# Whole-unit VectorE steps of 4096 columns in a fused linear-attention and rational-MLP kernel, with the split between engines and the written order changed

## Chip, cores and metric

One core of one Trainium2 chip. The metric is the device time in microseconds of one execution; a kernel is run several times and the median is taken. Five engines work side by side, each through its own queue in order: PE (TensorE, matrix products), DVE (VectorE, elementwise), ACT (ScalarE, activations and copies), POOL (GpSimd) and SP (SyncE, which here only issues DMAs). POOL also issues DMAs, those that add into their target among them.

## What is computed

The reference is two stages. The first is a gated linear recurrence for each of 4 batches and 8 heads, over 768 steps with head size 48:

```python
f = 1.0 / (1.0 + np.exp(-f_logit))
for t in range(S):
    state = f[:, :, t, :, None] * state + np.einsum('bhd,bhe->bhde', k[:, :, t], v[:, :, t])
    y[:, :, t] = np.einsum('bhd,bhde->bhe', q[:, :, t], state)
```

The second takes y as 3072 tokens of 384 numbers through a two-layer network whose activation is a rational function:

```python
h = x @ w_in                                  # 384 -> 2048
P = a[0] + a[1] * h + a[2] * h*h + a[3] * h*h*h
Q = 1.0 + np.abs(b[0]) * np.abs(h) + np.abs(b[1]) * h*h
out = (P / (Q + 1e-06)) @ w_out               # 2048 -> 384
```

## The kernel before

The work is cut into 12 units of 256 tokens: unit n is batch n mod 4, part n // 4 of the sequence, so a unit needs the state that unit n - 4 left. Each unit goes through the recurrence and then through the network. The hidden 2048 columns of the network are 16 blocks (m) of 128, so a unit's hidden layer is a tile of 128 partitions by 16 x 256 = 4096 columns. Steps take a range of blocks: `8 16` is one half (2048 columns), `0 4` a quarter (1024 columns).

There is no scheduler. A string, ORDER, lists some 860 steps by hand, and every engine gets its instructions in the order in which its steps stand in that string. Waits between engines follow from the data. So an engine that reaches a step whose input isn't there stops, and all later steps of that engine with it. The steps, with the engine and the line of the kernel before:

- Recurrence: `ld` loads (f, k, q issued by SP, v by POOL, L200); `ef`, `ls` exponential and logarithm of the gate (ACT, L278, L283); `cs` running sums (PE, L293); `A` their exponentials (ACT, L309); `xa` scaled k (1) and q (0) (DVE, L315); `T`, `Te` transposes and their copy (PE L327, ACT L337, once DVE L339); `sc`, `mk` scores and mask (PE L352, DVE L360); `vm` a rearranged piece of v (POOL, L367); `kv`, `si`, `ae`, `st` the new state (PE, PE, ACT, DVE, L421 to L449); `yb`, `yi` the output y (PE, L374), `ye` its copy to x (ACT, L439).
- Hidden layer: `h` products for four blocks (PE, L458; `ha`, `hb` the same in two parts, L482), `hy` their copy from PSUM to bf16 (ACT, L488).
- Denominator: `sq` h squared (DVE, L492; `sa` on ACT instead, L496), `ab` the absolute value, as a bit mask (DVE, L500). Their sum is formed in one of three ways: `u` by products with the identity in PSUM (PE, L508), `zv` by an add on DVE (L518), or `zd` by a DMA that adds (POOL issues it, L522). Then a logarithm, `ln` from u (ACT, L513) or `lz` from z (ACT, L526), and `ex`, an exponential that gives 1/Q in the tile qi (ACT, L530).
- Numerator: `p1`, `p2` two linear terms (DVE, L534, L539), `pm` p1 times h squared (DVE, L548), the sum of both by `tv` (DVE, L556) or by `ta`, a DMA that adds (POOL, L552), and `gm`, times qi (DVE, L560).
- Output: `o` products (PE, L570), `oe` copy (ACT or DVE, L577), `so` store (SP or ACT, L583).
- `dz k` issues k dummy products (PE, L302) whose result nobody reads.

PSUM is four slots of two banks; `@i` says which slot a step takes, and it waits until what was in the slot has been read. qi and lq (the logarithm) exist once for all units, z and h2 (the squares) twice, hy and the numerator's tile gall three times. `ld 2 f >mk.0.1` begins only behind step mk 0 1.

## Time and profile before

| | us |
|---|---|
| median of 3 runs | 218.3 |
| lowest and highest | 218.06, 219.33 |
| span of the profiled execution, first to last instruction | 216.3 |
| TensorE, VectorE, ScalarE, GpSimd busy | 203.2, 202.7, 200.8, 81.6 |

The profile has one execution; its own time is not listed apart from its span. The median is 2.0 us above the span. Matmuls are pipelined and their ends are modelled, so TensorE's busy time is an upper bound of the time it could not have done without. Instructions of VectorE and ScalarE overlap their neighbours a little: the time from one start to the next is shorter than the duration listed. The chain of waits is the work that ended last, followed back from the last instruction.

### The profile page before, as it was taken

The page shows a single profiled execution, that of the slowest core. Times are in us where ns is not written, and L with a number is a line of the kernel's source. Part 1 is how long each engine was busy: PE and PEld are TensorE (multiplying, and loading weights), DVE is VectorE, ACT ScalarE, POOL GpSimd, SP SyncE. Part 2 cuts the span into 40 slices and gives each one's busy share as a digit, 9 for nine tenths or more (in the row PEclk, how much of TensorE's full clock was granted, in tenths as well). Part 3 has the DMA queues.
Part 4 walks back from the last instruction along what each step waited for, and adds up shares of the span by engine and source line. Part 5 has one row for each costly group of instructions (what it writes and reads, how often), then busy time and mean ns, then how long its engine had stood idle before and what let it go on. Part 6 is the DMA issues. An engine that isn't in the chain of part 4 may idle for free.

```text
span 216.3 us, 7159 instructions
## 1 busy us (share of the span) xinstructions
PE 203.2 (94%) x3166; PEld 140.1 (65%) x3166; DVE 202.7 (94%) x246; ACT 200.8 (93%) x211; POOL 81.6 (38%) x91
## 2 busy tenths in 40 slices
PE   6989989699799999999999999999999999999993
PEld 2457658468377657658758658668668678676551
DVE  3588999999999999999999999999999999999991
ACT  4746899999999999999999999999999999999991
POOL 5250247120157803014954205954232516433300
PEclk9999999999999999999999999999999999999999
DMA  5999999999598999958999997999889793999863
GB/s 132 248 226 194 243 212 226 207 221 250 136 246 143 231 237 271 149 101 195 197 232 216 211 251 179 173 234 222 160 159 228 142 162 70 170 194 188 154 234 145
DMA packets 60910, 42.13 MB, mean 195 GB/s; under 512 B 51152, under 2 KB 54992, under 8 KB 60880
## 3 DMA queue, kind: packets, MB, share of 16 engines
q0 software_dynamic: 21232, 22.81, 66.0%
q1 hardware_dynamic: 39360, 18.68, 33.7%
q8 instruction: 24, 0.39, 0.7%
q10 hardware_dynamic: 288, 0.20, 0.3%
q14 instruction: 6, 0.05, 0.1%
HBM read 25.17 MB, written 4.72 MB: 138 GB/s over the span
## 4 chain that ended last, share of the span: by engine, by line
ACT 42%; DVE 21%; PE 18%; DMA 8%; issue 6%; POOL 3%; POOLq 0%; ACTq 0%; DVEq 0%
ACT qi L530 11%; ACT hy L488 10%; PE op L570 9%; ACT lq L526 8%; DMA fn<-in_f_logit_dram 4%; DMA z<-h 4%; PE warm L302 3%; DVE gall L548 3%; ACT A L309 3%; DVE scm L360 3%; DVE qkp L315 3%; PE hp L458 2%; DVE gall L560 2%; DVE gall L556 2%; ACT qkT L337 2%
## 5 line engine op out<-in xcount | busy, mean ns | idle before, releaser
L570 PE MATMUL op<-w_out_sb,gall 128*128 128x384 bf16 x384 | 70.1, 326 | 0.4 <-ACT hy L488 0.4
L458 PE MATMUL hp<-xT,w_in_sb 128*128 128x256 bf16 x564 | 65.3, 272 | 1.3 <-ACT xT L439 1.1
L458 PEld LDWEIGHTS <-w_in_sb 128*128 128x128 bf16 x564 | 55.0, 98 | 11.0 <-issue 2.8
L570 PEld LDWEIGHTS <-gall 128*128 128x128 bf16 x384 | 35.5, 98 | 23.6 <-DVE gall L560 0.9
L488 ACT CAST hy<-hp 128x1024 bf16<-128x1024 f32 x48 | 47.4, 1073 | 1.7 <-PE hp L482 1.2
L530 ACT ACTIVATE qi<-lq 128x2048 bf16<-128x2048 f32 (+1 forms) x26 | 46.9, 1845 | 0.0
L367 POOL COPY vmp<-vn 128x128 bf16<-128x128 bf16 x24 | 33.7, 1417 | 32.1 <-DMA vn<-in_v_dram 18.9
L526 ACT ACTIVATE lq<-z 128x2048 f32<-128x2048 bf16 (+1 forms) x20 | 36.9, 1846 | 0.6 <-DMA z<-h 0.5
L552 POOL DMA_DIRECT2D gall<-hy x17 | 14.8, 926 | 50.7 <-ACT A L309 11.5
L522 POOL DMA_DIRECT2D z<-h x18 | 17.3, 1065 | 36.3 <-issue 10.5
L560 DVE TENSOR_TENSOR gall<-gall,qi 128x2048 bf16<-128x2048 bf16 (+1 forms) x26 | 29.6, 1143 | 0.3 <-ACT qi L530 0.2
L548 DVE TENSOR_TENSOR gall<-gall,h 128x2048 bf16<-128x2048 bf16 (+1 forms) x26 | 29.4, 1138 | 0.0
L492 DVE TENSOR_TENSOR h<-hy 128x2048 bf16<-128x2048 bf16 (+1 forms) x26 | 27.3, 1059 | 1.5 <-ACT hy L488 1.4
L360 DVE TENSOR_TENSOR scm<-sc,mask 128x1024 bf16<-128x1024 f32 x24 | 28.4, 1211 | 0.0
L309 ACT ACTIVATE A<-cs 128x768 f32<-128x768 f32 (+1 forms) x26 | 19.6, 816 | 0.0
L500 DVE TENSOR_SCALAR z<-hy 128x2048 uint16<-128x2048 uint16 (+1 forms) x28 | 17.1, 618 | 0.1
L534 DVE TENSOR_SCALAR gall<-hy,a_sb 128x4096 bf16<-128x4096 bf16 (+1 forms) x14 | 16.9, 1210 | 0.2 <-ACT hy L488 0.2
L539 DVE TENSOR_SCALAR hy<-hy,a_sb 128x4096 bf16<-128x4096 bf16 (+1 forms) x14 | 16.6, 1184 | 0.0
L200 POOL DMA_DIRECT2D vn<-in_v_dram x12 | 13.2, 1104 | 2.2 <-PE y L374 2.2
L315 DVE TENSOR_TENSOR qkp<-kn,A 128x768 bf16<-128x768 f32 (+1 forms) x13 | 11.5, 887 | 2.0 <-ACT A L309 2.0
L278 ACT ACTIVATE fn<-fn 128x768 f32<-128x768 f32 (+1 forms) x13 | 10.7, 825 | 2.8 <-DMA fn<-in_f_logit_dram 2.7
L337 ACT COPY qkT<-tp 128x1024 f32<-128x1024 f32 (+1 forms) x12 | 12.5, 1041 | 0.7 <-PE tp L327 0.7
(72 smaller groups left out, 262.2 us busy)
## 6 DMA issues: line engine op xcount, KB each, us to landing
gall<-hy POOLq DMA_DIRECT2D x16, 512.0 KB, 6.7
z<-h POOLq DMA_DIRECT2D x15, 512.0 KB, 7.4
fn<-in_f_logit_dram SPq DMA_DIRECT2D x11, 384.0 KB, 7.4
kn<-in_k_dram SPq DMA_DIRECT2D x11, 384.0 KB, 9.8
qn<-in_q_dram SPq DMA_DIRECT2D x11, 384.0 KB, 7.2
out_dram<-osb SPq DMA_DIRECT2D x11, 384.0 KB, 4.1
vn<-in_v_dram POOLq DMA_DIRECT2D x12, 192.0 KB, 8.0
w_in_sb<-in_moe_w_in_dram POOLq DMA_DIRECT2D x4, 384.0 KB, 8.2
```

The source lines that it names most:

```text
L309: nc.scalar.activation(t, src, AF.Exp, scale=1.0 if x else -1.0)
L315: return nc.vector.tensor_mul(s["qk"][:, :, x, hh, 0:D], s["qk"[x]][:, hh].rearrange("p h i d -> p i h d"), A_sb[:, :, x].rearrange("p i ( ...
L360: return nc.vector.tensor_mul(t, s["sc", g].rearrange("s r a i t -> s (r a) (i t)"), mb)
L367: nc.gpsimd.tensor_copy(s["vm"][:, :, :, 32 * x:32 * x + 16], src)
L458: nc.tensor.matmul(t[:, m - m0, :], w_in_sb[:, kk, m * P:(m + 1) * P], s["x"][:, kk].rearrange("p i j t -> p (i j t)"), start=(kk == 0), s ...
L488: nc.scalar.copy(fl(big(s, "hy", "hy", 3), m0, m1), fl(s["hp", m0], 0, m1 - m0))
L492: return nc.vector.tensor_mul(fl(big(s, "h2", "h2", 2), m0, m1), fl(s["hy"], m0, m1), fl(s["hy"], m0, m1))
L526: nc.scalar.activation(fl(lq, m0, m1), fl(s["z"], m0, m1), AF.Ln, scale=regs[2], bias=1.0 + 1e-6)
L530: nc.scalar.activation(fl(qi, m0, m1), fl(lq, m0, m1), AF.Exp, scale=-1.0)
L548: return nc.vector.tensor_mul(fl(s["g"], m0, m1), fl(s["g"], m0, m1), fl(s["h2"], m0, m1))
L560: return nc.vector.tensor_mul(fl(s["g"], m0, m1), fl(s["g"], m0, m1), fl(qi, m0, m1))
L570: nc.tensor.matmul(s["op", j][:, j, 0:DM], s["g"][:, m, P * j:P * j + P], w_out_sb[:, m, :], start=(s["on", j] == 1), stop=(s["on", j] == KF))
```

## The change

All functions keep their work, except that `hy` and `ye` may now run on VectorE, which one step uses (`hy 11 4 8 v`). The rest is the ORDER string, which is written anew from the first to the last step. By kind of step and block range it differs so:

| step | before | after |
|---|---|---|
| `sq`, units 2 to 10 | 16 halves (2048 columns) | 9 whole units (4096) |
| `sa` (squares on ScalarE) | 4 quarters (units 2 and 4) | none |
| `ab`, `pm`, `gm`, units 2 to 10 | 18 halves each | 9 whole units each |
| `u` and `ln` | 11 quarters | 9 (unit 2's two are gone) |
| `lz` | 17 halves, 3 quarters | 18 halves, 3 quarters |
| `zd` (by DMA) | 15 halves, 3 quarters | 14 halves, 3 quarters |
| `zv` (on VectorE) | 2 halves (4, 6) | 4 halves (2, 3, 4, 6) |
| `ta` (by DMA) | 16 halves, 1 quarter | 20 halves, 1 quarter |
| `tv` (on VectorE) | 6 halves, 3 quarters | 2 halves, 3 quarters |
| `hy` on VectorE | none | 1 quarter (unit 11) |
| `dz`, in order | 9 5 4 3 1 2 1 1 | 1 4 2 9 1 5 3 1 |

`ex` stays at halves, `p1` and `p2` stay at whole units. In unit 2, blocks 0 to 8 had their denominator by `u`, and have it by `zd` now; blocks 8 to 16 had it by `zd`, and have it by `zv`.

The code, and of ORDER the first and the last lines:

```diff
 ORDER = """
-ld 0 f 2 4; cz 0; ab_ b a; cu 0; cz 1; ld 0 f 0 2; ld 1 f; ci; cu 1; ld 0 v; ld 0 k 0 2; ld 0 k 2 4; fa
-ld 0 q 2 4; ef 0 2 4; ls 0 2 4; cm; ef 0 0 2; dz 9 @2; cs 0 2 4 @2; fr; cz 3; ls 0 0 2; ld 0 q 0 2; ab_ a s
-ld 1 k; dz 5 @3; cs 0 0 2 @3; ef 1; ld 1 q; ls 1; vm 0 1; A 0 1 0 2; wi 12 16 >ls.1; dz 4 @0; cs 1 @0
-A 0 1 2 4; xa 0 1 0 2; A 0 0 2 4; wi 8 12; cz 2; A 0 0 0 2; xa 0 1 2 4; dz 3 @1; kv 0 @2; wi 4 8
-xa 0 0 0 2; si 0 0; ae 0; dz 1 @1; T 0 0 2 @1; wi 0 4; xa 0 0 2 4; st 0 0; Te 0 0 2 s; T 0 2 4 @3; A 1 1
-ld 1 v; Te 0 2 4; A 1 0; vm 0 0; sc 0 0 @1; si 0 1; mk 0 0; sc 0 1 @3; mk 0 1; ld 2 f >mk.0.1; ld 2 k
+ld 0 f 2 4; cu 1; cz 2; ld 0 f 0 2; cz 3; ld 0 k 2 4; cu 0; cz 0; ld 0 q 0 2; ld 0 k 0 2; ld 0 v; cm; ld 0 q 2 4
+ld 1 f; ci; ld 1 k; ld 1 q; ef 0 2 4; ab_ a s; ls 0 2 4; ab_ b a; ef 0 0 2; cs 0 2 4 @2; ls 0 0 2; A 0 1 2 4
+cs 0 0 2 @1; ld 3 f; dz 1 @3; xa 0 1 2 4; A 0 0 0 2; dz 4 @0; cz 1; A 0 1 0 2; A 0 0 2 4; xa 0 0 0 2; xa 0 1 0 2
+vm 0 0; T 0 0 2 @3; ld 1 v; kv 0 @0; xa 0 0 2 4; Te 0 0 2 s; fa; wi 4 8; T 0 2 4 @1; sc 0 0 @3; wi 0 4; ef 1
+Te 0 2 4; ae 0; ls 1; mk 0 0; sc 0 1 @2; cs 1 @1; wi 12 16 >ls.1; mk 0 1; si 0 0; vm 0 1; A 1 1; yb 0 0 2 @3
+st 0 0; fr; yb 0 2 4; ld 2 f >mk.0.1; A 1 0; vm 1 0; xa 1 1; ld 2 k; yi 0 1; wi 8 12; si 0 1; ld 2 q; xa 1 0
...
-zd 11 12 16; o 10 1 4 8; oe 9 0 2 s; p1 11 8 16; o 10 1 0 4; ex 11 4 8; tv 11 4 8; o 10 1 12 16; so 9 0 2 s
-p2 11 8 16; o 10 0 12 16; lz 11 8 12; gm 11 4 8; so 7 0 2 s; o 10 1 8 12; ex 11 0 4; pm 11 8 12
-o 10 0 8 12; pm 11 12 16; so 8 0 2 s; o 11 0 4 8 @1; ex 11 8 12; gm 11 0 4; o 11 1 4 8 @0; lz 11 12 16
-tv 11 8 12; o 11 1 0 4; gm 11 8 12; o 11 0 0 4; ex 11 12 16; tv 11 12 16; o 11 0 8 12; gm 11 12 16
-oe 10 0 2 s; so 10 0 2 s; o 11 1 8 12; o 11 0 12 16; oe 11 0 1 v; so 11 0 1 s; o 11 1 12 16; oe 11 1 2 s
+o 10 1 4 8 @0; ab 11 0 4; o 10 0 0 4; lz 11 12 16; p2 11 0 8; zd 11 0 4; o 10 1 8 12; pm 11 8 12; lz 11 8 12
+o 10 1 0 4; p2 11 8 16; o 10 0 8 12; ex 11 12 16; tv 11 4 8; ta 11 8 12; o 10 0 4 8; pm 11 12 16; oe 9 0 2 s
+o 10 1 12 16; gm 11 4 8; lz 11 0 4; o 10 0 12 16; so 9 0 2 s; tv 11 12 16; so 8 0 2 s; o 11 1 4 8 @2; ex 11 8 12
+gm 11 12 16; o 11 0 4 8 @1; pm 11 0 4; ex 11 0 4; o 11 0 12 16; gm 11 8 12; o 11 1 12 16; oe 10 0 2 s; tv 11 0 4
+o 11 1 8 12; gm 11 0 4; so 10 0 2 s; o 11 0 8 12; o 11 0 0 4; o 11 1 0 4; oe 11 0 1 v; so 11 0 1 s; oe 11 1 2 s
 so 11 1 2 a
 """
...
-    def hy(n, m0, m1):
+    def hy(n, m0, m1, eng="s"):
         s = unit(n)
-        nc.scalar.copy(fl(big(s, "hy", "hy", 3), m0, m1), fl(s["hp", m0], 0, m1 - m0))
+        (nc.scalar.copy if eng == "s" else nc.vector.tensor_copy)(
+            fl(big(s, "hy", "hy", 3), m0, m1), fl(s["hp", m0], 0, m1 - m0))
```

One unit of the middle, as its steps stand in the string (those on VectorE and ScalarE of unit 5's activation alone):

```diff
-ab 5 8 16; sq 5 8 16; sq 5 0 8; ab 5 0 8; p1 5 0 16; pm 5 8 16; pm 5 0 8; lz 5 8 16; p2 5 0 16
-lz 5 0 8; ex 5 0 8; ex 5 8 16; gm 5 0 8; gm 5 8 16
+ab 5 0 16; sq 5 0 16; p1 5 0 16; p2 5 0 16; pm 5 0 16; lz 5 0 8; lz 5 8 16; ex 5 0 8; ex 5 8 16; gm 5 0 16
```

147 lines of the change are left out of this document (71 added, 76 removed).

## The prediction

> **What bounds the kernel now.** I read the page's busy line first, then its chain, then busy time by stages.
>
> ```profile
> span 216.3 us, 7159 instructions
> PE 203.2 (94%) x3166; PEld 140.1 (65%) x3166; DVE 202.7 (94%) x246; ACT 200.8 (93%) x211; POOL 81.6 (38%) x91
> ACT 42%; DVE 21%; PE 18%; DMA 8%; issue 6%; POOL 3%; POOLq 0%; ACTq 0%; DVEq 0%
> ```
>
> Three engines are busy for 93 to 94% of the span, and the chain passes between them: no single one carries it. The stages tell more (columns: length, then busy time of PE, PEld, DVE, ACT, POOL with instruction counts, clock, DMA share, GB/s):
>
> ```profile
> 0.00:16.00 16.00, 13.33 (x170) 6.45 (x170) 9.31 (x35) 9.04 (x16) 7.75 (x20) 1.00 1.06 202
> 16.00:20.00 4.00, 3.87 (x66) 3.20 (x66) 3.27 (x8) 1.81 (x3) 0.00 (x0) 1.00 1.21 192
> 20.00:44.00 24.00, 21.47 (x357) 14.82 (x354) 23.50 (x30) 23.34 (x28) 9.08 (x13) 1.00 1.35 220
> 44.00:190.00 146.00, 141.94 (x2430) 101.41 (x2430) 145.06 (x147) 144.97 (x146) 59.70 (x52) 1.00 0.98 192
> 190.00:211.00 21.00, 20.83 (x142) 13.53 (x140) 20.74 (x30) 20.96 (x20) 5.09 (x6) 1.00 0.87 190
> 211.00:216.30 5.30, 1.79 (x11) 0.70 (x8) 0.82 (x2) 0.71 (x2) 0.00 (x0) 1.00 0.40 148
> ```
>
> From 20 to 211 us VectorE idles 0.50 + 0.94 + 0.26 = 1.7 us and ScalarE 0.66 + 1.03 + 0.04 = 1.7 us of 191; TensorE idles 2.53 + 4.06 + 0.17 = 6.8 us. So VectorE and ScalarE both run without gaps from the end of the start-up to the tail. The time is the start-up, plus the work of the fuller of these two, plus a tail of some 5 us. What an edit saves counts only if it shortens both, and what shortens one alone stops counting when the other is left as the bound. The median of the runs, 218.3, is 2.0 us above this span; I add 2.0 to every span below.
>
> **VectorE's work.** Prices are start to start, from pieces of the chain where instructions follow each other (start, time, what):
>
> ```profile
> 28.69 0.60 DVE h L492
> 29.29 0.34 DVE z L500
> 32.13 0.72 DVE hy L539
> 38.57 2.26 DVE h L492 x2
> 40.83 0.60 DVE z L500
> 52.85 1.13 DVE gall L556
> 56.78 2.26 DVE scm L360 x2
> ```
>
> A two-input step takes 0.60 us for 1024 columns and 2.26 / 2 = 1.13 for 2048: 0.53 per 1024 and 0.07 once. For 4096 that gives 4 x 0.53 + 0.07 = 2.19, against 2.26 for two halves. The one-input AND (L500) takes 0.34 and 0.60, so 0.26 and 0.08: 1.12 for 4096 against 1.20. No 4096-column form of either is in this trace; both are extended along a line. Then, for units 2 to 10:
> - pm and gm: each 18 halves to 9 wholes, 18 x 1.13 - 9 x 2.19 = 0.63 us less, twice: -1.26.
> - ab: 18 x 0.60 - 9 x 1.12 = 0.72 less.
> - sq: 16 halves (two halves were Squares on ScalarE) to 9 wholes: 19.71 - 18.08 = +1.63.
> - zv: two more halves, +2.26. tv: four halves fewer (units 0, 1, 1, 2, 3 to DMA; 7 back), -4.52.
> - hy of unit 11, blocks 4 to 8, comes to VectorE. Not in the trace; the bf16 copy from PSUM below took 0.69, the fp32 multiply from PSUM (L360) 1.13. I take 1.13, since this source is fp32 too.
>
> ```profile
> L339 DVE COPY qkT<-tp 128x1024 bf16<-128x1024 bf16 x1 | 0.7, 691 | 0.7 <-ACT qkT L337 0.7
> L492 DVE TENSOR_TENSOR h<-hy 128x2048 bf16<-128x2048 bf16 x18 | 21.9, 1225 | 0.6 <-ACT hy L488 0.4
> L492 DVE TENSOR_TENSOR h<-hy 128x1024 bf16<-128x1024 bf16 x8 | 5.4, 685 | 0.9 <-ACT hy L488 0.9
> ```
>
> Sum: -1.26 - 0.72 + 1.63 + 2.26 - 4.52 + 1.13 = -1.5 us. As pairs are merged 34 times, everything hangs on what a merge saves. The last two rows give durations: twice 685 less 1225 is 0.145 us, double the 0.07 by starts, because neighbours overlap by about 0.1. I take the starts. [...]
>
> **ScalarE's and TensorE's work.**
>
> ```profile
> 87.37 0.93 ACT h L496
> 88.30 1.82 ACT hy L488 x2
> L513 ACT ACTIVATE lq<-u 128x1024 f32<-128x1024 f32 x11 | 11.3, 1044 | 0.0
> L526 ACT ACTIVATE lq<-z 128x2048 f32<-128x2048 bf16 x17 | 33.6, 1979 | 0.6 <-DMA z<-h 0.5
> 200.49 0.94 PE u L508 x4
> ```
>
> ScalarE loses four Squares (4 x 0.93) and one copy (0.91): -4.6. Two logarithms of 1044 ns become one of 1979: nothing. TensorE loses the two u of unit 2, eight products of 0.94 / 4: -1.9. The 26 dummy products stay, but before, 25 of them ran ahead of unit 0's first hp product; now five (dz 1, dz 4) do, and 21 stand later, where one did: 20 x 0.218 (1.09 / 5, a row of the next part) = +4.4 in the dense part. So TensorE gains 2.5 us of work there against 6.8 us of idle: covered, as long as that idle lies where the dummies fall. VectorE is left as the bound, and -1.5 counts.
>
> **The start.** Steps are taken from the chain and the timeline:
>
> ```profile
> 1.80 4.04 PE warm L302 x9
> 6.67 1.09 PE warm L302 x5
> 6.88 0.84 ACT L278 ACTIVATE fn<-fn 128x768 f32<-128x768 f32 x1
> 7.76 0.84 ACT L283 ACTIVATE lsp<-fn 128x768 bf16<-128x768 f32 x1
> 8.51 1.61 ACT L309 ACTIVATE A<-cs 128x384 f32<-128x384 f32 x4
> 10.71 0.37 PE sv L421 x32
> 11.07 0.28 PE sv L427 x8
> 11.82 0.62 PE tp L327 x8
> ```
>
> ef 1 and ls 1 no longer stand ahead of the four A of unit 0: those begin near 6.9, not 8.51, and everything behind them could come 1.6 us sooner. Against it: the first nine dummies took 4.04 / 9 = 0.449 us each, the next five 1.09 / 5 = 0.218. TensorE begins at half pace, and the nine that bring it up to pace before the first cs are gone. At half pace the two halves of T cost 2 x 0.62 more, kv between them 0.37 + 0.28, and the first sc some 0.3: 2.2 us. Net +0.6. Bounds: -1.6 if TensorE is up to pace anyway, +2.2 if the earlier A doesn't help because q's and k's loads land no sooner.
>
> ```profile
> PEclk9999999999999999999999999999999999999999
> ```
>
> The row of the granted clock shows full pace throughout, so it doesn't separate these; the durations do. [...]
>
> On the queues: POOL now issues v of unit 1 ahead of w_in; h of unit 0 takes blocks 4 to 8 first, whose w_in is now issued first, so they wait on one 384 KB transfer as before. SP issues f of unit 3 early, ahead of f of unit 2, which still waits for mk.0.1. I put these at nothing: h of unit 0 cannot begin before its own x, which comes about as late as before.
>
> **The tail.**
>
> ```profile
> z<-h POOLq DMA_DIRECT2D x3, 256.0 KB, 4.3
> gall<-hy POOLq DMA_DIRECT2D x16, 512.0 KB, 6.7
> L526 ACT ACTIVATE lq<-z 128x1024 f32<-128x1024 bf16 x3 | 3.3, 1093 | 0.0
> L530 ACT ACTIVATE qi<-lq 128x1024 bf16<-128x1024 f32 x4 | 4.2, 1089 | 0.0
> 91.11 3.60 ACT qi L530 x2
> 201.43 11.38 PE op L570 x68
> ```
>
> Unit 11's quarters come in the order 4, 12, 8, 0, and ab of quarter 0 is late. From its end to the last gm VectorE has nine 1024-column steps and two p2 of 2048: 9 x 0.60 + 2 x 0.72 = 6.8 us. In that time zd must land (4.3) and lq, the exponential of quarter 8 and that of quarter 0 must run (3 x 1.09): 7.6, less some overlap. +0.4, bounds 0 and +0.8. Behind the last gm follow two groups of output products, as before.
>
> Three more accumulating transfers of 512 KB (four ta more, one zd less) take 6.7 us each, issued on POOL, which is busy for 38%; where the order puts other work between issue and use they are hidden, and I see no place but the tail where it doesn't.
>
> **Sum.** 216.3 - 1.5 + 0.6 + 0.4 = 215.8, and with 2.0: **217.8**. New waits in the middle I take at nothing over today's 1.7 us; they can lie 1.7 lower and, by the third rival, some 5 higher.
>
> **Rivals.** About 1%, 2.2 us, is what a measurement here can tell from no change: under 216.1 counts as faster, over 220.5 as slower.
> - Faster: the merges save 0.145 rather than 0.07 (34 x 0.075 = 2.5 less), or the start comes 1.6 early (-2.2 against my +0.6), or most of today's 1.7 us of VectorE waits goes because ScalarE now runs 4.6 ahead. One of these gives about 215.2. For it: the durations. Against it: the starts, and that today's few waits leave little to win. 0.24, all of it under 216.1.
> - TensorE becomes the bound: if its 6.8 us of idle lie where nothing can be put, the time changes by its own work, +2.5, plus 2.2 of half pace: 218.3 + 4.7 = 223.0. It decides from the point where less than half of the idle can be used. Against it: the rows show 2.5 us of idle between 20 and 44, near whose end eleven dummies now fall. 0.11.
> - The whole steps gate ScalarE, slower: gm on 4096 columns needs both halves of qi, and holds both until it ends, so the next unit's first exponential waits for 2.2 us of gm where it waited for 1.13, and gm starts up to 1.8 (3.60 / 2) later. ScalarE's 4.6 us of spare cover 0.5 a unit. If VectorE, which has no spare, waits 0.5 us in each of nine units: +4.5, so 217.8 + 4.5 = 222.3. It decides from 0.3 us a unit. For it: every such step is longer than any VectorE step before. Against it: a twelfth of ScalarE's 200.8 us is 16.7, so beside its two exponentials a unit gives it 13 us of other steps to run meanwhile. 0.17.
>
> **Chances.** My case keeps 0.48: within 1%, its terms' bounds reach from 216.2 to 220.4. Faster 0.24, the two slower cases together 0.28. The range runs from 215.0, below the middle of the fast case, to 221.5, into the slow ones, and leaves out about a fifth.
>
> **What would show it.** In the new profile: 4096-column two-input steps near 2.3 us long and 2.19 apart; VectorE's busy sum near 201.2 and ScalarE's near 196; VectorE idle between 20 and 211 us still under 2.5 us and ScalarE's near 5; unit 0's A before 7.2 us and transposes at 0.15 us each; lq of unit 11's last quarter waiting for z's transfer. Wrong would be: VectorE waiting for qi or for hp or sc in the middle (a rival holds), or TensorE with less than 3 us of idle there.

## The result and the profile after

| us | before | after |
|---|---|---|
| median of 4 runs | 218.44 | 224.53 |
| lowest to highest | 218.06 to 219.33 | 223.79 to 226.99 |
| profiled execution: its time, its span | –, 216.3 | 224.98, 223.3 |

The ratio is 1.0282, 95% interval 1.0208 to 1.0356: slower, by about 6 us. 217.8 was forecast, 215.0 to 221.5. Ratios leave out disturbed runs and the medians here don't, so the two can differ a little in what follows.

The page after (span, busy time, the granted clock in 40 slices, the chain by engine):

```profile
span 223.3 us, 7123 instructions
PE 204.9 (92%) x3158; PEld 143.3 (64%) x3158; DVE 200.6 (90%) x211; ACT 196.9 (88%) x205; POOL 78.9 (35%) x94
PEclk9998899999999999999999997999999999999998
PE 35%; ACT 13%; issue 5%; DMA 4%; DVE 4%; POOL 0%; ACTq 0%; DVEq 0%
```

VectorE does 2.1 us less work than before, ScalarE 3.9 less, and the span is 7.0 longer. So the time is in waits, and it must be asked in which stretch. Busy time by stages, before (columns: length, then PE, PEld, DVE, ACT, POOL with counts, clock, DMA share, GB/s):

```profile
0.00:30.00 30.00, 26.57 (x421) 15.96 (x421) 22.08 (x55) 20.19 (x30) 9.97 (x24) 1.00 1.16 211
30.00:60.00 30.00, 26.60 (x477) 18.74 (x477) 30.00 (x33) 29.89 (x35) 9.30 (x13) 1.00 1.20 208
60.00:120.00 60.00, 58.51 (x903) 42.05 (x898) 59.23 (x60) 59.42 (x61) 27.16 (x21) 1.00 1.01 202
120.00:140.00 20.00, 19.65 (x323) 13.41 (x323) 19.93 (x22) 20.00 (x21) 8.86 (x7) 1.00 1.03 196
140.00:211.00 71.00, 70.11 (x1056) 49.25 (x1055) 70.64 (x79) 70.62 (x67) 26.33 (x28) 1.00 0.91 179
```

and after:

```profile
0.00:30.00 30.00, 21.05 (x387) 14.61 (x388) 18.05 (x49) 15.70 (x25) 9.15 (x23) 0.94 1.12 197
30.00:60.00 30.00, 29.44 (x525) 20.67 (x523) 29.96 (x35) 29.55 (x37) 11.24 (x15) 1.00 1.23 242
60.00:120.00 60.00, 59.83 (x1035) 43.11 (x1034) 60.00 (x52) 59.82 (x64) 27.62 (x24) 1.00 1.09 209
120.00:140.00 20.00, 17.95 (x307) 12.83 (x304) 17.00 (x14) 16.37 (x18) 8.97 (x8) 0.91 0.97 185
140.00:211.00 71.00, 68.70 (x877) 47.83 (x866) 68.99 (x55) 69.64 (x58) 21.11 (x25) 1.00 0.88 172
```

Since VectorE's work and its idle time make up the span, the difference can be booked on it. VectorE's idle time changes by +4.03 (0 to 30), +0.04, -0.77, +2.93 (120 to 140) and +1.65 us (140 to 211). Behind 211 us it idles 216.3 - 211 - 0.82 = 4.48 before and 223.3 - 211 - 6.57 = 5.73 after (work there from the same view): +1.25. Together +9.13, less 2.1 of work: +7.0. Two stretches carry 7 of the 9: the first 30 us, and 120 to 140.

**The two stretches.** TensorE's timeline after (start, time, line, what, how many; in brackets the idle time before it and what ended it):

```profile
18.03 0.33 PE L419 MATMUL sv<-ind,lsp 128*128 128x2 bf16 x7
20.43 0.16 PE L419 MATMUL sv<-ind,lsp 128*128 128x2 bf16 x1 [2.08 <-issue]
...
21.14 1.91 PE L319 MATMUL tp<-ident,qkp 128*128 128x128 bf16 x16
...
23.16 1.91 PE L453 MATMUL hp<-xT,w_in_sb 128*128 128x256 bf16 x12
...
130.04 0.28 PE L366 MATMUL y<-scm,vmp 64*32 64x128 bf16 x5
132.37 0.23 PE L366 MATMUL y<-scm,vmp 64*32 64x128 bf16 x3 [2.05 <-issue]
...
132.75 2.28 PE L453 MATMUL hp<-xT,w_in_sb 128*128 128x256 bf16 x12
```

In the midst of eight equal products of `kv` of unit 1, and again in the midst of eight equal products of `yb 8 0 2`, TensorE does nothing for 2 us, and the profile names no engine, no semaphore and no data transfer that ended the wait ("issue"). These are stall 1 and stall 2 below. Behind each of them products run at half pace: twelve hidden products take 2.28 us at 132.75 and 1.91 at 23.16, where the same twelve took 1.47 before. The clock shows it (two windows of after):

```profile
20.60:24.00 3.40, 3.14 (x22) 2.54 (x22) 1.62 (x4) 1.86 (x4) 0.00 (x0) 0.50 1.20 206
133.30:136.70 3.40, 3.40 (x18) 2.26 (x16) 1.31 (x2) 2.00 (x3) 0.14 (x1) 0.50 1.03 230
```

VectorE stands for the state that these products lead to (its timeline):

```profile
21.38 1.02 DVE L444 TENSOR_TENSOR state<-sv,alast 128x384 bf16<-128x384 f32 x2 [2.86 <-PE sv L424]
135.39 0.56 DVE L444 TENSOR_TENSOR state<-sv,alast 128x384 bf16<-128x384 f32 x1 [3.00 <-PE sv L424]
```

The first stretch holds more than stall 1. Unit 0's first hidden products start at 23.16; before it was this row:

```profile
16.99 1.47 PE L482 MATMUL hp<-xT,w_in_sb 128*128 128x256 bf16 x12
```

6.2 us later, then, though VectorE's first mask step began a little sooner than before (13.53 against 13.69). Until 16 us hardly anything is lost (VectorE has worked 8.96 us by then against 9.31); the loss comes between the scores of unit 0 and its hidden layer, where the new order puts the state and transposes of unit 1. The four loads of w_in by issue (its rows in before, then in after: duration, first and last start) and from issue to landing:

```profile
L206 POOL DMA_DIRECT2D w_in_sb<-in_moe_w_in_dram x4: 757/766/769, 9.7 to 11.9; - x4
DMA to landing us min/median/max: 5.7/8.2/10.6
```

```profile
L198 POOL DMA_DIRECT2D w_in_sb<-in_moe_w_in_dram x4: 741/763/775, 12.2 to 17.7; - x4
DMA to landing us min/median/max: 8.1/9.9/10.9
```

The first w_in piece is asked for 2.5 us later and the last 5.8 later, so of the hidden layer's weights none lands before 12.2 + 8.1 = 20.3. Three things thus stand ahead of unit 0's hidden products: unit 1's state and transposes on TensorE, with stall 1 in their midst; `ae 1` ahead of `ye 0` on ScalarE; and these loads. That is read from the order and the landings; the runs of the second and fourth groups below take it apart in part.

**The whole steps themselves** came out as priced (groups by form, after):

```profile
L556 DVE TENSOR_TENSOR gall<-gall,qi 128x4096 bf16<-128x4096 bf16 x9 | 20.6, 2286 | 0.8 <-ACT qi L526 0.7
L544 DVE TENSOR_TENSOR gall<-gall,h 128x4096 bf16<-128x4096 bf16 x9 | 20.5, 2283 | 0.0
L496 DVE TENSOR_SCALAR z<-hy 128x4096 uint16<-128x4096 uint16 x9 | 11.0, 1219 | 0.6 <-ACT hy L483 0.6
```

2.28 us long; start to start in the timeline it is 2.20 to 2.21. And `gm` waited for qi once, 0.7 us in nine units.

**Why TensorE stops in the midst of equal products.** The DMA view has a queue for instructions:

```profile
q8 instruction: 24, 0.39, 0.7%
```

24 fetches, 0.39 MB, 16 KB each: the instruction stream comes in blocks. By the count they are TensorE's: 3158 products and as many weight loads are 6316 instructions, some 263 to a fetch. Between the two stalls TensorE's records count (a window from one to the other)

```profile
20.30:132.20 111.90, 108.80 (x1917) 77.92 (x1916) 108.86 (x107) 107.67 (x120) 46.60 (x44) 0.98 1.13 214
```

1917 products and 1916 weight loads, 3833; with the 7 semaphore instructions of its queue in between, which count as no engine's work, 3840. In the same window the DMA view's row of fetches counts 15 of them (0.25 MB). So a block is 3840 / 15 = 256 instructions, and both stalls stand at the same place of one. The trace has the fetches' times too: the block of stall 2 is fetched at about 130, when a window of half a microsecond around it (129.7 to 130.2) shows it beside accumulating transfers,

```profile
q0 software_dynamic: 22, 0.09, 95.0%
q8 instruction: 1, 0.02, 11.7%
```

and used 2.41 us after its fetch began (129.96 to 132.37), that of stall 1 2.22 (18.21 to 20.43), and no block of after sooner. From the entry of the block ahead to the fetch's begin, counted in blocks from the stalls, it is 4.1 to 5.3 us in after for the fetches at 18, 25, 32, 61, 97, 130 and 137 us, where loads or accumulating transfers fill the DMA engines (share 1.07 to 1.47 in the microsecond around each), and under 1 us, or the fetch even begins before the block is entered, for those at 86, 101, 111, 143 and 149. Of these five the engines are far from full only at 101 and 149 (0.65 and 0.06, against 1.00 to 1.87 at the others), so full engines didn't delay every fetch. The blocks ahead of stalls 1 and 2 were done 4.6 and 4.8 us after they were entered, sooner than delay and fetch together, 6.65 and 6.87; of the others 20 lasted 5.86 us or more, and one of 3.72 was entered after the next one's fetch had begun, and none has such a gap behind it. Ahead of stall 2 lie `yi 8`, `yb 8 2 4` and `kv 9`, all of short products, so its block ran out first. In before no fetch came less than 2.78 us ahead of its use, and there is no such stall. This is the theory called F below: late blocks cost the time. Its rivals: the whole steps themselves cost it (W: they hold buffers and delay what stands behind them on VectorE), or the start does, by TensorE's half pace without the nine dummies (C: unit 0's first eight transposes took 1.03 us, 0.62 in before) or by its order of loads and steps.

### The profile page after: what moved, and what is told of

It is laid out like the page before. It is cut to its first block, busy times and chain, and to the rows that moved or that the text cites. A ratio compares the mean times of both kernels' runs of the same rounds, so it can differ in the third digit from the quotient of the medians.

```text
span 223.3 us, 7123 instructions
## 1 busy us (share of the span) xinstructions
PE 204.9 (92%) x3158; PEld 143.3 (64%) x3158; DVE 200.6 (90%) x211; ACT 196.9 (88%) x205; POOL 78.9 (35%) x94
## 4 chain that ended last, share of the span: by engine, by line
PE 35%; ACT 13%; issue 5%; DMA 4%; DVE 4%; POOL 0%; ACTq 0%; DVEq 0%
PE op L566 15%; PE hp L453 12%; ACT qi L526 5%; DMA z<-h 4%; ACT lq L522 3%; ACT hy L483 3%; PE y L366 2%; PE tp L319 2%; DVE gall L556 2%; PE cs L285 1%; DVE scm L352 1%; PE sc L344 1%; ACT osb L573 1%; PE warm L294 1%; DVE h L488 1%
## 5 line engine op out<-in xcount | busy, mean ns | idle before, releaser
L453 PE MATMUL hp<-xT,w_in_sb 128*128 128x256 bf16 x564 | 69.8, 277 | 0.6 <-ACT hy L483 0.5
L566 PE MATMUL op<-w_out_sb,gall 128*128 128x384 bf16 x384 | 68.6, 326 | 1.5 <-DVE gall L556 1.3
L522 ACT ACTIVATE lq<-z 128x2048 f32<-128x2048 bf16 (+1 forms) x21 | 38.7, 1851 | 0.5 <-DMA z<-h 0.3
L548 POOL DMA_DIRECT2D gall<-hy x21 | 20.4, 1032 | 46.5 <-PE y L366 14.8
L359 POOL COPY vmp<-vn 128x128 bf16<-128x128 bf16 x24 | 24.8, 1084 | 33.3 <-DMA vn<-in_v_dram 27.2
L556 DVE TENSOR_TENSOR gall<-gall,qi 128x4096 bf16<-128x4096 bf16 (+2 forms) x17 | 28.2, 1658 | 1.2 <-ACT qi L526 0.7
L488 DVE TENSOR_TENSOR h<-hy 128x4096 bf16<-128x4096 bf16 (+2 forms) x19 | 28.4, 1505 | 0.0
L544 DVE TENSOR_TENSOR gall<-gall,h 128x4096 bf16<-128x4096 bf16 (+2 forms) x17 | 28.1, 1655 | 0.1
L444 DVE TENSOR_TENSOR state<-sv,alast 128x384 bf16<-128x384 f32 x20 | 10.9, 549 | 7.1 <-PE sv L424 7.1
L329 ACT COPY qkT<-tp 128x1024 f32<-128x1024 f32 (+1 forms) x12 | 12.2, 1020 | 4.6 <-PE tp L319 4.6
L496 DVE TENSOR_SCALAR z<-hy 128x4096 uint16<-128x4096 uint16 (+2 forms) x19 | 15.7, 824 | 0.6 <-ACT hy L483 0.6
L285 PE MATMUL cs<-lsp,Ui 128*128 128x384 bf16 (+1 forms) x39 | 11.1, 344 | 5.2 <-ACT lsp L275 5.2
```

The lines of the kernel that those rows point to most:

```text
L359: nc.gpsimd.tensor_copy(s["vm"][:, :, :, 32 * x:32 * x + 16], src)
L453: nc.tensor.matmul(t[:, m - m0, :], w_in_sb[:, kk, m * P:(m + 1) * P], s["x"][:, kk].rearrange("p i j t -> p (i j t)"), start=(kk == 0), s ...
L488: return nc.vector.tensor_mul(fl(big(s, "h2", "h2", 2), m0, m1), fl(s["hy"], m0, m1), fl(s["hy"], m0, m1))
L522: nc.scalar.activation(fl(lq, m0, m1), fl(s["z"], m0, m1), AF.Ln, scale=regs[2], bias=1.0 + 1e-6)
L544: return nc.vector.tensor_mul(fl(s["g"], m0, m1), fl(s["g"], m0, m1), fl(s["h2"], m0, m1))
L548: nc.gpsimd.dma_start(out=fl(s["g"], m0, m1), in_=fl(s["hy"], m0, m1), accum_op=ALU.add)
```

## Experiments

Eighteen kernels. Each but a_burst, which ran once, carries its ratio to before with the 95% interval; the expectations, quoted, were written before it ran. To shift where blocks end, a step was added that computes nothing that is read; it issues k products of two columns:

```diff
+    def dt(k, sl):
+        t = slot(sl, [P, 2, 512], F32, "tiny")
+        for i in range(k):
+            nc.tensor.matmul(t[0:UB, 0, 0:UB], ind, ind, start=True, stop=True, skip_group_check=True)
```

Each product is two instructions (a weight load and a product: c_layout's 70 bring both counts from 3158 to 3228), so `dt 24` shifts all later block ends by 48.

### First group: moving the block ends

**a_tiny24, a_tiny72, a_tiny104**: after, with 24, 72 or 104 such products in front.

```diff
-ef 0 0 2; cs 0 2 4 @2
+ef 0 0 2; dt 24 @0; cs 0 2 4 @2
```

> Theory F (fetch): TensorE's instructions come in blocks of 256, and the two stalls of 2 us of the changed kernel are two blocks that came late, because the 256 instructions before them were run in under 6.9 us while data transfers held the fetch back by 4.4 us. Theory C: the cold start (the nine warm-up products gone) costs it. Theory W: the whole-unit steps of 4096 columns cost it. Here 24 tiny products (48 instructions, [2 x 2] results that nobody reads) stand at the front of TensorE's order, where it idles. F: every boundary now falls 48 instructions earlier in the work; by the trace of the changed kernel the quickest blocks then end at 17.8, 52.7, 66.1, 127.5 and 168.7 us, so the stalls stay or move: no row that waited at 18.4 or at 130.3 us waits at the same product, others do, 222 to 228 us. C and W: nothing moves, 224.5 +- 0.7 us, with the two stalls in front of the same two products.

> 72 tiny products (144 instructions) in front instead of 24. F: the boundaries fall 144 instructions earlier, where nearly every block takes over 5.6 us of work; one quick block ends at 43 us (3.2 us). The stalls at 18 and 130 us go, at most one of about 1 us appears near 43 us, and the time is 217 to 219.5 us. C: the tiny products are no warm-up of the pace that nine 512-column products are, 223.5 to 225 us. W: 224.5 +- 0.7 us.

> The changed kernel with 104 tiny products (208 instructions) in front; they end before the first sum needs TensorE. By the measured delays and the times of the blocks this is the worst place for the boundaries: stalls of 0.7 to 2 us near 22, 26, 90 and 113 us and one of 4 us or more near 128 us, in the run of small products of units 8 and 9. F: 225 to 231 us. C and W: 224.5 +- 0.7 us.

| kernel | median us | ratio | span | TensorE's gaps by "issue" over 0.5: end (length) |
|---|---|---|---|---|
| after | 224.53 | 1.0282 [1.0208, 1.0356] | 223.3 | 20.4 (2.08), 132.4 (2.05) |
| a_tiny24 | 222.41 | 1.0226 [1.0182, 1.0270] | 219.2 | 68.6 (1.60) |
| a_tiny72 | 224.76 | 1.0289 [1.0237, 1.0340] | 223.8 | 48.2 (1.75), 138.5 (1.59) |
| a_tiny104 | 224.89 | 1.0298 [1.0245, 1.0352] | 223.8 | 28.3 (1.83), 118.1 (1.10), 135.3 (2.10) |

The old gaps go in every case, and new ones open, at the same place mod 256 again. That settles where the gaps come from. It doesn't settle what they cost: the best of the three still has one of 1.60, and the other two are no faster than after. That 72 would leave at most 1 us of gaps was wrong, and so was the gap of 4 us or more that 104 was to open near 128 us: which block is short of time can't be told from the order alone, since the delay of the fetch varies between none and over 5 us.

**a_dz9**: nine dummy products moved from unit 1's activation to the front.

```diff
-ef 0 0 2; cs 0 2 4 @2
+ef 0 0 2; dz 9 @0; cs 0 2 4 @2
...
-A 4 1; dz 9 @3; ta 0 8 16
+A 4 1; ta 0 8 16
```

> The changed kernel with its nine 512-column dummy products moved from about 48 us to the front of TensorE's order, as the kernel before had them. C: the transposes of unit 0 run at full pace again (half their 1.03 us for 8), most of the loss is regained, 217 to 220 us. F: up to 48 us the boundaries fall 18 instructions earlier, which is still inside kv of unit 1, so stall 1 stays some products earlier, and past 48 us they lie where they were within one instruction, so stall 2 stays in yb of unit 7: 223 to 225 us. W: 224.5 +- 0.7 us.

224.25, ratio 1.0273 [1.0225, 1.0321], span 222.5. Stall 1 is gone (up to where the nine stood, block ends lie 18 instructions elsewhere), which F had not expected; stall 2, behind that place, stays, 2.11 up to 131.7. The first transposes run at full pace again (eight in 0.62), and unit 0's hidden products start at 18.96 rather than 23.16. Yet the time is after's, not the 217 to 220 of C. VectorE gains 2.5 us in the first 30; behind gaps of 1.29 and 0.50 at 48 us, where the nine were taken away, the clock is at half from 50.2 to 53.6.

**b_tiny32**: before, with 32 such products in front (and one constant formed earlier, which they read).

```diff
-ef 0 0 2; dz 9 @2; cs 0 2 4 @2
+ef 0 0 2; dt 32 @0; dz 9 @2; cs 0 2 4 @2
```

> The kernel before with 32 tiny products (64 instructions) in front of its nine dummy products (and the two-column indicator that they multiply set first on VectorE instead of later). F: the boundaries fall 64 instructions earlier, where by its trace the quickest blocks end at 144, 175 and 189 us after 4.3, 4.6 and 3.8 us of work, against 5.9 us at the least as it stands: stalls of 0.5 to 1.5 us appear there and the kernel loses 0.5 to 4 us, 219 to 222 us. C and W: no change, 218.4 +- 0.7 us.

218.30, ratio 0.9996 [0.9975, 1.0017]; its longest gap by "issue" is 0.48, at 17.2, at the same place mod 256. A miss: moving the block ends in the order of before opened none of the stalls that were expected at 144, 175 and 189 us. So with the old order late blocks cost nothing here, at either of two placings; why, whether it has fewer runs of short products beside full DMA engines, wasn't tested.

**c_layout**: after, with 30, 8 and 32 such products at three places, meant to put every block end where its block is long.

```diff
-ef 0 0 2; cs 0 2 4 @2
+ef 0 0 2; dt 30 @0; cs 0 2 4 @2
...
-A 4 1; dz 9 @3
+A 4 1; dt 8 @3; dz 9 @3
...
-p2 1 0 16; T 4 @0
+p2 1 0 16; dt 32 @0; T 4 @0
```

> The changed kernel with tiny products put in at three places of TensorE's order: 30 in front, 8 before the nine dummy products at 48 us, 32 before the transposes of unit 4 at 52 us. The places were worked out from the traces so far: at the same time of the work the fetch of a block started the same time after the block before it was entered, whatever kernel it was (about 4 us late at 16 to 26 us, 2 at 34 to 43, 4 at 59 to 66, 0 at 98, 4.5 at 123 to 134, 0 at 138 to 146), and a block was never used within 2.2 us of the start of its fetch; with these places every block has more work before it than its fetch takes, but for two that miss by under 0.5 us. F: no TensorE gap over 0.8 us without a wait, VectorE idle after 30 us under 4 us in sum, 216.5 to 218.5 us. C and W (cold start or whole steps cost it): 223 to 225 us, since all of those are as they were.

224.60, ratio 1.0235 [1.0184, 1.0286]. A miss too, in the range that C and W gave: gaps of 1.07 up to 54.4, 0.81 up to 97.1 and 1.64 up to 138.1.

### Second group: why the block is late, and what a clean run is worth

**a_noacc**: after, without five accumulating transfers between 119 and 127 us (four sums of the numerator, of units 4 and 5, and one of the denominator, of unit 5, are left out).

```diff
-ta 4 0 8
...
-ta 4 8 16
-zd 5 8 16
...
-ta 5 8 16
...
-ta 5 0 8
```

> The changed kernel without the five accumulating DMAs that are issued between 119 and 127 us (numerators of units 4 and 5, half of unit 5's denominator: these sums are left out, and the output of those units is not the reference's). TensorE's instructions and their blocks stay the same. F with the fetch queued behind data transfers: the fetch that started 4.46 us after its block before was entered at 125.5 us starts under 2 us after it, and the stall of 2.05 us in front of the same product in y of unit 8 is gone or under 0.5 us, with the half-pace products after it: 219.5 to 222.5 us. If the lateness of the fetch does not come from these transfers (a fixed rhythm of the sequencer): the stall stays at 2 us, 223.5 to 225 us.

224.0, ratio 1.0257 [1.0208, 1.0307]. TensorE's timeline where stall 2 was, the only row of the DMA view at the block's fetch (126.8 to 127.3), and VectorE's stages:

```profile
131.01 0.22 PE L366 MATMUL y<-scm,vn 64*32 64x128 bf16 x2
131.16 1.48 PE L453 MATMUL hp<-xT,w_in_sb 128*128 128x256 bf16 x12
```

```profile
q8 instruction: 1, 0.02, 16.6%
```

```profile
0.00:30.00 30.00, 20.85 (x386) 14.21 (x387) 17.72 (x49) 15.46 (x25) 9.91 (x24) 0.77 1.15 202
120.00:140.00 20.00, 19.93 (x335) 14.78 (x333) 20.00 (x17) 19.98 (x22) 2.11 (x3) 1.00 0.39 90
140.00:211.00 71.00, 67.74 (x849) 46.56 (x848) 67.73 (x54) 67.72 (x57) 21.22 (x25) 0.98 0.85 164
```

Same order of TensorE, same block end, nothing else on the DMA engines: the fetch begins 0.86 us after its block is entered instead of 4.46, the stall is gone, the twelve products take 1.48 again, and VectorE idles 0.00 us between 120 and 140 instead of 3.00. So the late block of stall 2 is a fetch that stands behind data. The time hardly falls, though: 1.26 of the 3 us are lost again behind 140 (3.27 idle against 2.01), 0.33 in the first 30, where the two kernels are the same, and the profiled span is 0.9 shorter. What a removed stall is worth at its place isn't what the end gains. The time missed the 219.5 to 222.5 that was expected; stall 1 stands there as in after, 2.20 long.

**a_burst**: after, with one step of long hidden products put between the runs of short ones.

```diff
-yb 8 2 4; xa 10 1; kv 9 @0; ab 6 0 16; yb 8 0 2; h 7 12 16 @3
+yb 8 2 4; xa 10 1; h 7 12 16 @3; ab 6 0 16; yb 8 0 2; kv 9 @0
```

> The changed kernel with one thing moved on TensorE and no product added: the hidden-layer products of unit 7's last quarter (12 long products) go ahead of, and the state products of unit 9 (40 small ones) behind, the second half of unit 8's y products. F: the block that ends in the second stall then holds 24 instructions of long products in place of small ones and takes 5.5 to 5.8 us instead of 4.8 us of work; with the delay of 4.46 us and 2.2 us of fetch the stall shrinks from 2.05 to 0.9 to 1.2 us, and the half pace after it need not come; it stands in front of another product, the one with the same place in its block. If the block were not what is waited for, the gap would stay at its product or go with it.

One run: 222.0, span 220.0. The stall is now in `kv 9`, at the same place of the block:

```profile
130.54 0.24 PE L413 MATMUL sv<-vn,qkp 64*64 64x48 bf16 x5
131.66 0.40 PE L413 MATMUL sv<-vn,qkp 64*64 64x48 bf16 x27 [0.88 <-issue]
```

With 1.48 us of products more in the block it falls from 2.05 to 0.88: the block's length against the fetch's delay, 4.46 us in after, decides, as F has it.

**d_layout**: after, with 11, 16 and 6 short products at places chosen from the fetch times of the traces so far; **d_burst** is d_layout with the long step of a_burst ahead of `kv 9`.

```diff
-ef 0 0 2; cs 0 2 4 @2
+ef 0 0 2; dt 11 @0; cs 0 2 4 @2
...
-pm 5 0 16; T 8 @1
+pm 5 0 16; dt 16 @1; T 8 @1
...
-tv 7 8 16; T 11 @2
+tv 7 8 16; dt 6 @2; T 11 @2
```

> Tiny products at three other places, worked out with the delays of all traces so far and with the times of the work as they are when no stall comes ahead: 11 in front (22 instructions), 16 before the transposes of unit 8 at 119 us, 6 before those of unit 11 at 160 us. F: no block comes over 0.6 us late; no TensorE gap over 0.8 us without a wait; what is left late is the start (first k and q, w_in and f of unit 3: VectorE idle up to 30 us 7 to 9 us in sum); 217.5 to 220.5 us. If whole steps or the new order in the dense part cost time of their own (W), the loss stays: 223 us or more with no stalls to see.

> The run before this, and the hidden-layer products of unit 7's last quarter put in front of the state products of unit 9, into the run of 256 small products that the second stall followed. F: the block there takes 1 us longer, the last lateness (0.5 us near 134 us) goes: the same as the run before it or up to 0.7 us less. W: no difference.

d_layout: 223.05, ratio 1.0267 [1.0220, 1.0314], span 220.3, and no gap by "issue" over 0.42. d_burst: 224.11, 1.0282 [1.0245, 1.0318], no gain, with a gap of 1.72 up to 171.7. d_layout is the cleanest test of F on the whole time: its stages, and a row of TensorE's waits,

```profile
0.00:30.00 30.00, 21.35 (x400) 14.54 (x401) 18.95 (x50) 16.41 (x26) 9.07 (x23) 0.89 1.14 201
120.00:140.00 20.00, 19.54 (x342) 14.37 (x340) 19.67 (x17) 19.33 (x21) 8.90 (x8) 1.00 0.98 185
```

```profile
PE sv L418 <- DMA vn<-in_v_dram: 2.1, 1, 2.1
```

Between 120 and 140 VectorE idles 0.33 instead of 3.00, nearly as in before (0.07). The profiled span is 3.0 us shorter than after's, but it is the fastest of six executions (222.07 to 225.53); of the medians' difference, 1.5, no more can be said than that it points the same way, since the two intervals overlap. F had 217.5 to 220.5, so it missed; W had "223 us or more with no stalls to see", and that is what came. Late blocks aren't the whole loss, then.

The first 30 us are nearly as poor as in after (11.05 idle against 11.95). TensorE, which comes to `kv 1` sooner here, waits 2.1 us for v of unit 1, which lands at 17.78, and the clock is at half from 17.0 to 23.9. In after v had landed at 17.4, before `kv 1` began, so stall 1 didn't hide that load. What stall 1 and half pace cost at this place is seen in the kernels that have neither there. From the start of `kv 1` to the first hidden product it takes 5.5 us in after (17.66 to 23.16), 3.5 in d_layout (17.92 to 21.42), but 2.2 in a_tiny24 (17.25 to 19.45) and in c_layout (17.56 to 19.77). The first 30 us of these two:

```profile
0.00:30.00 30.00, 20.15 (x417) 13.85 (x418) 20.65 (x51) 17.51 (x27) 9.70 (x23) 0.94 1.16 204
0.00:30.00 30.00, 21.35 (x427) 14.38 (x428) 20.88 (x52) 17.88 (x28) 9.54 (x23) 0.94 1.13 200
```

VectorE idles 9.35 and 9.12 us there, and 9.1 to 10.2 in a_tiny72, a_dz9 and c_split, which have no stall 1 either, against 11.95 in after and 7.92 in before. **So late blocks, with the half pace behind them, go with the middle stretch, some 3 us of the 7, and with 1.8 to 2.9 of the 4 us at the start; the other 1.2 to 2.3 of these 4 stay in those kernels too.** That is read from single traces by stages; no kernel with the new order is free of late blocks and half pace from end to end, and none has the time back. The nearest by its profiled span is a_tiny24, 219.2, its fastest execution.

### Third group: the whole steps alone

**c_split**: c_layout, with every whole `sq`, `ab`, `pm` and `gm` of units 2 to 10 cut into its halves, at its place.

```diff
-pm 4 0 16
+pm 4 0 8; pm 4 8 16
```

> The run before this with the four whole-unit steps (square, absolute value, product with the squares, product with the inverse) of units 2 to 10 each split into two adjacent halves: 36 more VectorE instructions, nothing else. The prediction's terms (0.07 to 0.08 us saved by each merge, start to start) give 36 x 0.07 to 0.08 = 2.5 to 2.9 us longer VectorE work, and so 1.5 to 3 us more than the unsplit one where VectorE stays the bound. W (whole steps hold ScalarE and TensorE up): faster than the unsplit one.

226.73, ratio 1.0341 [1.0290, 1.0393]: about 1% more than c_layout beside it, 2.1 us by the medians, as the merges' price had it. Busy, c_layout and then c_split:

```profile
PE 203.8 (91%) x3228; PEld 142.5 (64%) x3228; DVE 202.7 (91%) x211; ACT 197.6 (88%) x205; POOL 74.1 (33%) x94
```

```profile
PE 204.1 (91%) x3228; PEld 142.5 (64%) x3228; DVE 204.2 (91%) x247; ACT 198.2 (88%) x205; POOL 75.9 (34%) x94
```

36 instructions more cost VectorE 1.5 us of busy time. Against two halves at the same place, the whole steps are a gain in the new order; that the longer step itself loses the time is refuted.

**b_pm**: before, with the ten `pm` of units 1 to 10 whole, at the place of the second half. **b_merge**: before, with 25 of the pairs whole (8 `pm`, 7 `sq`, 5 `ab`, 5 `gm`), where the second half stood near.

```diff
-pm 1 8 16; ex 1 0 8; h 2 8 12 @3; xa 3 0; h 2 0 4 @0; pm 1 0 8
+ex 1 0 8; h 2 8 12 @3; xa 3 0; h 2 0 4 @0; pm 1 0 16
```

> The kernel before with only the ten products with the squares of units 1 to 10 made whole-unit steps (10 instructions of 2048 columns fewer), in the place of the second half. By the prediction's term (0.07 to 0.08 us each) 0.7 to 0.8 us less VectorE work: 217.3 to 218.0 us. If a longer step in itself makes the short steps behind it late (the masks that TensorE waits for), the gain is lost or turned: 218.5 to 221 us.

> The kernel before with the whole-unit steps alone: 25 pairs of halves (7 squares, 5 absolute values, 8 products with the squares, 5 products with the inverse) that stand near each other in its order become one step each, nothing else moves, TensorE's order and its blocks stay. By the prediction's terms VectorE saves 25 x 0.07 to 0.08 = 1.8 to 2.0 us: 216.2 to 217.2 us. If whole steps make ScalarE or the DMAs wait (W): 218.5 us or more.

b_pm: 220.24, ratio 1.0099 [1.0072, 1.0127], span 217.5, clock full throughout. b_merge: 224.72, 1.0297 [1.0264, 1.0329], span 221.8, clock full. In b_pm the merge pays what was forecast: start to start the `pm` take 2 x 1.184 + 10 x 2.210 = 24.47 us where 22 x 1.143 = 25.15 stood, 0.068 a merge. And yet it is slower; TensorE now has waits for VectorE that before hasn't (its waits):

```profile
PE sv L415 <- DVE qkp L309: 1.3, 2, 1.1
PE y L368 <- DVE scm L354: 1.2, 1, 1.2
```

The scaling step of the first row stands behind a whole `pm` on VectorE and comes 1.06 us later than behind a half. The mask of the second row is 0.7 us late, but for another reason: between 100.9 and 106.7 us VectorE's steps ran slower, one scaling step above all, which took 1.62 us where it takes 0.95 in before,

```profile
100.91 1.62 DVE L309 TENSOR_TENSOR qkp<-kn,A 128x768 bf16<-128x768 f32 x1
```

and a GpSimd copy beside it, from 100.98 on, stands in before too (from 101.19, beside the same step). Why it was slow is open. By the whole trace VectorE's idle time grows by only 0.5 us, to 14.1, and its busy time by 0.7 instead of falling by that much. In b_merge VectorE itself waits, since a whole `sq` or `ab` needs the last of four copies from PSUM (VectorE's waits, and a stage):

```profile
DVE z L493 <- ACT hy L481: 3.4, 3, 1.6
DVE h L485 <- ACT hy L481: 3.1, 4, 1.6
```

```profile
140.00:211.00 71.00, 66.37 (x1031) 47.07 (x1031) 66.40 (x62) 66.94 (x62) 28.44 (x29) 1.00 0.88 165
```

4.6 us of idle where before had 0.36, 6.4 more over the whole span. So whole steps in the old order cost 2 us (ten of them) to 6 us (25); with 25 it is waits, with ten only in part. That an order written anew is what they want is argued from this, not shown: the change's own is slower too.

### Fourth group: the start

All five go out from d_layout, which has neither stall 1 nor stall 2. **d_warm** puts dummies into TensorE's gaps at the start, so that the clock holds; **d_v1** issues v of unit 1 earlier; **d_warmv1** does both; **e_f3** is d_warmv1 with f of unit 3, its gate and its logarithm later; **e_start** is e_f3 with `si 0 0` ahead of `cs 1` as well.

```diff
-ef 0 0 2; dt 11 @0; cs 0 2 4 @2
+ef 0 0 2; dt 3 @0; cs 0 2 4 @2
...
-mk 0 0; sc 0 1 @2
+mk 0 0; dz 3 @2; sc 0 1 @2
...
-ld 3 k; kv 1 @2
+ld 3 k; dz 5 @2; kv 1 @2
```

```diff
-vm 0 0; T 0 0 2 @3; ld 1 v; kv 0 @0
+ld 1 v; vm 0 0; T 0 0 2 @3; kv 0 @0
```

```diff
-cs 0 0 2 @1; ld 3 f; dz 1 @3
+cs 0 0 2 @1; dz 1 @3
...
-ld 2 q; xa 1 0
+ld 2 q; ld 3 f; xa 1 0
...
-mk 1 0; ef 3; h 0 0 4 @0; mk 1 1; ls 3
+mk 1 0; h 0 0 4 @0; mk 1 1
...
-hy 1 12 16; cs 3 @0
+hy 1 12 16; ef 3; ls 3; cs 3 @0
```

```diff
-sc 0 1 @2; cs 1 @1; wi 12 16 >ls.1; mk 0 1; si 0 0
+sc 0 1 @2; si 0 0; cs 1 @1; wi 12 16 >ls.1; mk 0 1
```

> d_layout with 8 of the 11 tiny products in front replaced by 512-column dummy products where TensorE idles at the start: 3 before the second half of unit 0's scores, 5 before the state products of unit 1, which wait for v; the count of instructions ahead of every later block is the same. Theory H (half pace): the granted clock stays at 1.00 up to 30 us, the transposes of unit 1 take 1.0 us instead of 1.91 and the hidden products 1.3 instead of 2.66: VectorE idle up to 30 us falls from 10.7 to 8 to 9 us, 220.5 to 222 us. Theory V (the load): the state products still begin at 17.5 to 18.5 us; no gain over 0.5 us.

> d_layout with the load of v of unit 1 put ahead of the copy of unit 0's v in GpSimd's order, so that it is issued near 4.5 us instead of 9.6 to 11.3. V: v of unit 1 lands by 13 us, its state products begin near 16 us with no wait for it; the loads of unit 0's k and q land up to 1 us later in exchange; net 1 to 2 us less, 221 to 222 us. H: begins earlier, but still at half pace: less than 1 us.

> Both edits of the two runs before. If the load and the half pace both cost, their gains add up: 2.5 to 4 us less than d_layout, 219 to 220.5 us, with VectorE idle up to 30 us near 7 to 8 us as in the kernel before. If w_in, which lands at 20 us and later, is next behind them, the gain stops at 1 to 2 us and TensorE waits for w_in at 20 us.

> d_warmv1 with the load of f of unit 3 and its two ScalarE steps put later: the load behind q of unit 2, the steps in front of that unit's sums. Loads hold the start: w_in's first pieces land 1 to 2 us earlier, ScalarE no longer waits for f at 24 us, VectorE idle up to 30 us falls from 9.8 to 8 to 9 us: 1 to 2 us less than d_warmv1 (whose runs were 221.3 to 224.7). If something else holds it: no change beyond 0.5 us.

> The run before this, and the first identity product of unit 0's state put ahead of unit 1's sums on TensorE, which wait for f of unit 1: the state of unit 0 (VectorE waits 1.4 us for it at 16 us) comes about 1 us earlier; 0.5 to 1 us less than the run before it if nothing else is late there, no change if the masks or v are.

| kernel | median us | ratio | unit 0's hidden products from | VectorE busy by 60 us |
|---|---|---|---|---|
| before | 218.44 | | 16.99 | 52.1 |
| after | 224.53 | 1.0282 [1.0208, 1.0356] | 23.16 | 48.0 |
| d_layout | 223.05 | 1.0267 [1.0220, 1.0314] | 21.42 | 48.95 |
| d_warm | 224.57 | 1.0291 [1.0239, 1.0343] | 20.28 | 49.4 |
| d_v1 | 226.24 | 1.0219 [1.0147, 1.0291] | 19.98 | 47.5 |
| d_warmv1 | 223.82 | 1.0260 [1.0218, 1.0302] | 21.52 | 49.7 |
| e_f3 | 225.36 | 1.0282 [1.0236, 1.0327] | 21.85 | 46.1 |
| e_start | 225.77 | 1.0349 [1.0304, 1.0395] | 21.98 | 47.05 |

None regains the start. d_warm holds the clock at 1.00 from end to end, and VectorE idles 9.58 us in the first 30 instead of d_layout's 11.05, so half pace costs up to 1.5 us there (v of unit 1 also landed 0.8 sooner); 1.0 of it is lost again by 60 us, where a late block makes a gap of 0.96 up to 55.3, and a gap of 1.57 up to 172.0 follows, since its products move block ends too. The median gains nothing. In a_noacc, above, half pace lies over `kv 1` as well, and VectorE idled only 0.33 more than in after. In d_v1, whose trace is of a long execution (227.87; its four are 221.85 to 228.8), v of unit 1 lands at 13.5 and `kv 1` waits no more, but begins at 17.77 all the same, and then unit 3's gate, which lands at 25.0, holds ScalarE, and VectorE stands behind it (VectorE's waits):

```profile
DVE h L493 <- ACT hy L488: 2.6, 1, 2.6
```

e_f3 takes that load back, and q of unit 1 (2.2 us, up to 19.4) and the running sums (2.6 us between 34 and 37) are late instead. Each edit lifts one wait, and the next load in the queue stands in its place. By 60 us every one of these has done 2.4 to 6 us less of VectorE's work than before. So what late blocks and half pace leave of the start's loss is one of the order, of loads against first uses. One sign of it: in d_warm, as in a_dz9 and c_split, the first hidden products wait for w_in, 0.2 to 0.6 us, which lands between 18.9 and 20.2 there and at 15.4 in before. Which part belongs to `kv 1`, to `ae 1` ahead of `ye 0` and to w_in's later issue stays open. Moving unit 0's `ye` and hidden products ahead of unit 1's state, the edit that the landings suggest, wasn't tried.

None of the eighteen is faster than before.

## Why the prediction was wrong

| term, us | predicted | measured |
|---|---|---|
| VectorE's work | -1.5 | -2.1 |
| start: up to the first mask step | +0.6 | -0.2 (13.53 against 13.69; its idle time is in the next row) |
| start: queues and unit 0's hidden layer | 0 | +4.0 (all of VectorE's idle time up to 30 us) |
| new waits in the middle | 0, bounds -1.7 and +5 | +3.9 (30 to 211 us) |
| tail | +0.4 | +1.3 (behind 211 us) |

**Right.** "For 4096 that gives 2.19": 2.20 to 2.21 measured, 0.068 saved a merge in b_pm against 0.07, and c_split shows that it counts in the new order. Durations give more, 2 x 1.221 - 2.283 = 0.159 us; start to start less than half of that is saved, and it is starts that add up. ScalarE's -4.6 measured -3.9, TensorE's +2.5 measured +1.7. The A of unit 0 began at 5.52, before 7.2 as said. Half pace at the start was right for the first products (eight transposes at 9.75 took 1.03, 0.13 each), though the granted clock is listed as 1.00 there. What it cost by the first mask step isn't shown: A came 3.0 us sooner and the mask 0.16, but VectorE also waited 1.6 us for k and 0.9 for q, and in a_noacc, whose order is the same there, the mask came at 12.28.

**The steps that failed.** There are two. First: "I put these at nothing: h of unit 0 cannot begin before its own x, which comes about as late as before." x came later: its copy began at 20.71 instead of 15.53, since it and unit 0's hidden products had been put behind unit 1's state and transposes, and a late block with half pace behind it fell into these; w_in was issued 2.5 to 5.8 us later. The prediction followed unit 0 to its scores and stopped; each queue should have been followed to the first hidden product, with the landings of that trace. It cost 4 us of VectorE's time, the largest term, of which 1.8 to 2.9 are gone in the kernels without that block and half pace; the rest is the order. Second: "New waits in the middle I take at nothing over today's 1.7 us". The range's bound of 5 would have held it, but the cause that was thought of, a gate on ScalarE, isn't the one: 2.9 of the 3.9 us are the late block in `yb 8 0 2`, with its half pace behind it. The prediction has no term for instructions that come late, and nothing in the profile of before shows such a wait. Most of the rest are three VectorE waits of 0.6 to 0.7 behind 140 us (for qi, for scores, for a copy of h).

**The rivals.** "The whole steps gate ScalarE" has its wait, for qi, once and at 0.7 us, not 0.5 in each of nine units. "TensorE becomes the bound", 223.0, came nearest by its figure and not by its mechanism: TensorE's work grew by 1.7 us, and its idle time up to 211 us didn't fill, it grew from 9.6 to 14.0; it stood waiting and then ran at half pace. "Faster" counted on waits that ScalarE's lead would remove; instead VectorE's idle time between 30 and 211 us rose from 1.2 to 5.1. Its other two grounds failed as well: a merge saves 0.068, and the first mask step came 0.16 sooner. Two of its sums don't come out either: the third ground alone gives 217.8 - 1.7 = 216.1, not 215.2, and the bounds of start and tail reach from 215.2 to 219.8, not from 216.2 to 220.4.

**The tail.** "lq of unit 11's last quarter waiting for z's transfer" didn't show: that step, at 212.7, found its data there. The tail is longer by small waits among the last quarters and by 0.9 behind the last `gm`, where the last store lands 2.7 us after its issue instead of 1.9.

**What stays open.** The medians of the kernels with the new order lie between 222.0 and 226.7, with spreads between their own runs mostly of 2 to 5 us (d_v1: 7), while before's thirteen runs in one set lie within 2.0. Removing a gap of 2 us shows in the stage where it stood, and only about as much as the spread in the median. How the rest of the start's loss is shared out, and how much of the run-to-run spread is a matter of where the late blocks fall, wasn't settled.
